# Two second-layer steps split by high and low parts, and Relus, casts and subtractions of the first tiles reordered

## The chip, the core and the metric

The kernel runs on one core of a Trainium2 chip. The core has five engines with queues of their own, each working in order: TensorE (PE, matrix products into PSUM; PEld are its weight loads), VectorE (DVE), ScalarE (ACT), GpSimd (POOL) and SyncE (SP, which here issues every DMA). They wait for each other by semaphores alone. The metric is the device time of one execution in microseconds; less is better.

## What is computed

A window attention with 8 batches, 8 heads, 576 positions and head width 64, and behind it a feed-forward layer of 4608 tokens:

```python
scores = scale * np.matmul(q, k.transpose(0, 1, 3, 2))
mask = (rel >= 0) & (rel < 64)
attn = softmax(np.where(mask, scores, -1e9))
x = np.matmul(attn, v)          # (4608, 512)
h = x @ w_in                    # 512 -> 2048
r = np.maximum(h, 0.0)
g = r * r
return g @ w_out                # 2048 -> 512
```

The weights arrive as 64-bit numbers, which the kernel reads as two 32-bit words each and turns into 32-bit ones.

## The kernel before

Twelve tiles of 384 tokens. The first four are "plain" tiles; the change lies in the first two (t = 0 and 1), whose work is interleaved with loading and converting the weights. All of it is one program in straight line, in an order written out by hand: the string `order` holds tokens such as `M11` or `p10a`, an operation's letter, a number, and sometimes the engine (d VectorE, a ScalarE, p GpSimd). A loop walks through the string and issues each token's instructions, so the string sets the order in every engine's queue. From tile 2 on a planner sets the order, and the change does not touch it.

To have enough precision, every 32-bit operand of a matmul is split into a high part (a rounded cast) and a low part (the number minus the high part), and a product is three: high by high, high by low, low by high.

The operations, with their lines:

- Weight block f (128 of the 2048 columns; 16 blocks): `w` fetches it (L105, L107); `a` takes the absolute value of the upper words (ScalarE, L121); `b` clamps and shifts it (VectorE, two instructions, L123 and L124); `c` and `d` put in the lower words and the sign (VectorE, L126, L128); `h` casts to the high part (ScalarE, L132); `l` subtracts it for the low part (VectorE, L135). The blocks use two staging buffers `a` in turn: `a` of block f can run when `l` of block f-2 is done.
- Step n = (tile, block): 34 steps in an order that `steps` holds. `M` is the first layer's product, 12 matmuls into PSUM bank 4 (L407), always the same bank. `r` is the Relu from that bank into one of two buffers `r` (ScalarE, L416), `p` the square in place (ScalarE here, L419), `g` the cast to the high part into one of three buffers (ScalarE, L424), `G` the subtraction for the low part into one of two buffers (VectorE, L426). `O` is the second layer's product, 9 matmuls of 512 columns into three banks (`mm2`, L445 to L450): first three with (high, high), then three with (high, low), at the end three with (low, high), so only the last three need `G`. `i` and `I` are an `O` in two pieces.
- So M of one step can begin when r of the step before has emptied bank 4; r of step n when G of step n-2 has read the buffer; G of step n when O of step n-2 has read the low half.
- Attention of a section i (a third of a tile): `S` scores (TensorE, L238), `o`, `s` mask, `z`, `y` maximum, `e`, `f` exponentials (ScalarE, L266), `k`, `R`, `m` division by the sum (`m` on GpSimd, L275), `X` transposes (TensorE, L279), `x` into SBUF, `V` values (TensorE, L301), `H` and `Q` high and low part of x. `T`, `U` transpose q and k of the first positions (TensorE, L199), `t`, `u` copy the result (L205). U2 and U3 use the same bank, so U3 needs u2 done.

Of the kernel before, what the change touches and what calls it, by code (L numbers as in the profile page):

```python
# [29 lines left out]
def window_attention_relu2_ffn(ctx: ExitStack, tc: tile.TileContext, q, k, v, w_in, w_out, out):  # L30
# [399 lines left out]
    def in_turn(x):  # L430
        return x.rearrange("p (a b) -> p b a", a=2)
# [49 lines left out]
    steps = [(t, f) for t in range(2) for f in range(AHEAD)]  # L481
    n0 = n1 = AHEAD
    while n1 < NF:
# [8 lines left out]
        L0 K5 P0 L1 P1 T1 t1d T0 t0a J0 j0 Y0 S0 o0a T2 t2a s0 z0 y0d T3 t3d J1 L2 K2 S1 j1 e0 o1a T4 t4a v0 w1 Y1 L3 v1  # L492
        N0 f0 K2 T5 d0 k0p t5a h0 s1 K5 z1 y1d S2 R0 m0d e1 l0 o2a X0 K5 x0 V0 s2 f1 k1p T6 z2 w2 R1 a1 b1 m1p X1 H0a Q0
        c1 t6a v2 L4 N1 y2p K2 f2 T7 t7a x1 S3 e2 d1 o3a s3 V1 k2p R2 U0 z3 h1 H1a u0a K4 l1 Q1
        m2p X2 U1 x2 w3 v3 a2 b2 K3 c2 y3p f3 u1a V2 T8 T9 H2a Q2 t8a t9a d2 S4 e3 o4a k3d R3 h2 s4 M0 U2 r0 u2a l2 p0a v4 z4
        U3 u3a a3 m3p X3 x3 b3 g0 G0 M1 c3 r1 p1a y4p S5 o5a w4 v5 s5 d3 f4 e4 w5 w6 g1 G1 V3 H3a k4p R4 z5 Q3
        h3 l3 a4 M2 r2 p2a O0 b4 O1 w7 v6 m4p X4 x4 c4 M3 g2 G2 V4 y5p e5 f5 k5p r3 H4a p3a g3 R5 d4 h4 a5 Q4
        w8 O2 G3 l4 m5p X5 x5 M4 a6 V5 w9 w10 w11 i3 r4 p4a g4 b5 H5d Q5 b6 M5 I3 r5 p5a c5 d5 w12 M6 w13 G4 O4
        h5 g5 r6 p6a c6 g6 M7 w14 d6 h6 w15 v7 v8 G5 O5 l5 r7 p7a a7 q0 M8 G6 O6 g7 l6 a8 r8 M9 b7 c7 d7 h7 G7 r9 O7
        p8a g8 p9a g9 M10 b8 c8 d8 G8 O8 l7 h8 r10 M11 l8 G9 a9 p10a g10 O9 a10 r11 p11a b9 c9 b10 M12 g11 G11  # L500
        O11 G10 r12 p12a M13 O10 q1 B0 c10 d9 h9 g12 d10 h10 r13 p13a l9 l10 a11 M14 a12 G12 r14 O12 M15 b11 B1
        B2 c11 B3 g13 G13 p14a r15 d11 h11 g14 O13 b12 c12 B4 M16 G14 p15a g15 r16 d12 h12 O14 p16a g16 l11 a13
        B5 B6 B7 l12 G15 M17 r17 a14 p17a O15 M18 G16 O16 b13 c13 r18 M19 d13 b14 g17 G17 O17 c14 h13 p18a l13
        g18 G18 O18 d14 r19 M20 a15 p19a b15 g19 G19 h14 l14 r20 O19 c15 d15 p20a g20 M21 G20 B8 B9 D0 q2 O20 h15 l15 r21
# [45 lines left out]
    with tc.manual_schedule(engines={E.PE, E.DVE, E.Activation, E.Pool, E.SP}):  # L550
        for token in order.split():
            op, eng = token[0], token[-1] if token[-1] in "dap" else None
            n = int(token[1:].rstrip("dap"))
            if op in "LN":
                load_first("LN".index(op), n)
            elif op == "v":
                load_v(*divmod(n, (NB + 1) // 2))
            elif op == "w":
                fetch_w(n)
            elif op == "q":  # L560
                load_qk(1 + n // NPAIR, n % NPAIR)
            elif op == "D":
                turn(1 + n // NPAIR, n % NPAIR)
            elif op in "TU":
                ps_f[op, n] = turn_first("TU".index(op), *divmod(n, 2))
            elif op in "tu":
                copy_first("tu".index(op), *divmod(n, 2), ps_f[op.upper(), n], copier(eng))
            elif op == "K":
                idle(n)
            elif op == "P":  # L570
                fetch_w(0, n)
            elif op in "JjY":
                weight("abc"["JjY".index(op)], 0, half=n)
# [694 lines left out]
    for s in range(NP * FULL + 2):  # L1268
        if s < NP * FULL:
            for mark in marks.get(2 * s, []):  # L1270
                mark()
            for n in range(7):
# [3 lines left out]
                if s < LAST and s % 2 == 0 and n % 2 == 0 or s == FAST_END + 1 and n % 2 == 0:  # L1276
                    f = s // 2 * 2 % NP * 2 + n // 2
# [61 lines left out]
```

## Time and profile before

| | |
|---|---|
| median of 3 runs | 840.22 us (840.2 to 841.16) |
| the profiled execution | 841.01 us, its span 839.3 us |
| TensorE busy | 825.5 us, 98% of the span |
| VectorE busy | 620.4 us, 74% |
| ScalarE busy | 434.8 us, 52% |
| GpSimd busy | 242.7 us, 29% |
| mean granted TensorE clock | 0.998 of full speed |

The span goes from the first to the last instruction; the execution's own time is a little longer. Busy times are averages over stages with different limits: the first 100 us are the stage that the change touches. Matmuls are pipelined, so that the events of one engine overlap a little; the start of an event minus the start of the one before is what a group of matmuls really takes.

### The profile page before, as it was taken

Reading aid. Unit: us, or ns where it says so; the run is one execution under the profiler, and the core shown is the slowest. Engines: PE = TensorE matmul, PEld = TensorE weight load, DVE = VectorE, ACT = ScalarE, POOL = GpSimd, SP = SyncE. Lnnn points to the kernel's source line nnn. Section 1 sums busy time; section 2 is a strip of 40 time slices with the busy share of each in tenths; the row PEclk is TensorE's granted clock in tenths of the full one; section 3 lists DMA queues with packets and bytes.
Section 4 is the critical chain, followed back from the end, with each engine's and each line's share of the span. In section 5 each row is a group of like instructions: output and inputs, shape, how many; then the busy total and the mean of one; then the engine's idle time right before and its main releaser. Section 6 shows DMA issues by size and latency. Waiting matters only on the chain.

```text
span 839.3 us, 18283 instructions
## 1 busy us (share of the span) xinstructions
PE 825.5 (98%) x6926; PEld 763.5 (91%) x6926; DVE 620.4 (74%) x908; ACT 434.8 (52%) x1181; POOL 242.7 (29%) x313
## 2 busy tenths in 40 slices
PE   8799999999999999999999999999999999999998
PEld 6689899889999999999999999999999999999997
DVE  6999997567656867867777866788766769566876
ACT  6796774656447554544452455344355425455441
POOL 1220003014647520311251334252233462202121
PEclk9999999999999999999999999999999999999999
DMA  9999945737598884999897898999895766889742
GB/s 225 246 343 273 357 176 88 140 116 182 142 197 259 219 175 114 312 243 219 180 307 235 215 229 175 260 289 231 272 286 151 256 213 183 250 263 309 242 168 76
DMA packets 292264, 184.99 MB, mean 220 GB/s; under 512 B 191184, under 2 KB 257488, under 8 KB 290128
## 3 DMA queue, kind: packets, MB, share of 16 engines
q1 hardware_dynamic: 292176, 183.81, 78.9%
q8 instruction: 55, 0.90, 0.5%
q14 instruction: 33, 0.27, 0.1%
HBM read 142.87 MB, written 40.89 MB: 219 GB/s over the span
## 4 chain that ended last, share of the span: by engine, by line
PE 92%; ACT 3%; DVE 3%; issue 1%; DMA 0%; SPq 0%; POOL 0%; ACTq 0%; DVEq 0%; POOLq 0%
PE banks L940 26%; PE banks L1038 24%; PE banks L407 14%; PE banks L449 13%; PE banks L1189 5%; PE banks L238 4%; PE banks L301 3%; PE banks L279 2%; ACT sel L266 1%; ACT a L121 1%; DVE a L126 1%; DVE w L135 0%; DMA w<-in_k_dram 0%; PE banks L199 0%; DVE a L123 0%
## 5 line engine op out<-in xcount | busy, mean ns | idle before, releaser
L1038 PE MATMUL banks<-w 128*128 128x512 f32 x888 | 199.8, 381 | 0.0
L1038 PEld LDWEIGHTS banks<-w 128*128 128x128 f32 x888 | 165.9, 189 | 21.6
L407 PE MATMUL banks<-x,w 128*128 128x384 f32 x768 | 138.9, 331 | 0.4 <-ACT r L416 0.3
L449 PE MATMUL banks<-w,g 128*128 128x512 f32 x576 | 136.1, 382 | 0.0
L407 PEld LDWEIGHTS banks<-x,w 128*128 128x128 f32 x768 | 127.2, 190 | 5.1 <-ACT r L416 2.0
L940 PE MATMUL banks<-x,w 128*128 128x384 f32 x768 | 130.3, 326 | 0.0
L940 PEld LDWEIGHTS banks<-x,w 128*128 128x128 f32 x768 | 125.6, 189 | 0.0
L449 PEld LDWEIGHTS banks<-w,g 128*128 128x128 f32 x576 | 106.4, 189 | 13.3 <-issue 0.3
L266 ACT ACTIVATE sel<-sel,nm 128x64 f32<-128x64 f32 x272 | 90.8, 336 | 22.6 <-DVE nm L260 22.2
L940 PE MATMUL banks<-w 128*128 128x384 f32 x576 | 100.7, 329 | 0.0
L970 POOL TENSOR_TENSOR g<-g 128x384 f32<-128x384 f32 x48 | 46.5, 972 | 181.5 <-ACT g L981 173.6
L940 PEld LDWEIGHTS banks<-w 128*128 128x128 f32 x576 | 93.4, 189 | 1.6
L1045 DVE TENSOR_TENSOR w<-w,banks 128x512 f32<-128x512 f32 (+1 forms) x61 | 41.1, 677 | 41.7 <-PE banks L1038 41.5
L416 ACT ACTIVATE r<-banks 128x384 f32<-128x384 f32 x64 | 31.1, 487 | 66.7 <-PE banks L407 61.2
L275 POOL TENSOR_TENSOR sel<-sel,nm 128x512 f32<-128x512 f32 x33 | 37.3, 1130 | 83.3 <-ACT g L981 32.8
L539 POOL TENSOR_TENSOR a<-w 128x256 f32<-128x256 f32 x28 | 24.3, 886 | 104.5 <-DVE w L135 74.7
L426 DVE TENSOR_TENSOR g<-r,g 128x384 fp32r<-128x384 f32 x64 | 38.2, 600 | 21.4 <-ACT g L424 14.6
L1022 ACT CAST w<-w 128x512 fp32r<-128x512 f32 x37 | 23.0, 621 | 56.4 <-PE banks L1038 56.4
L266 ACT ACTIVATION_READ_ACCUMULATOR sel<-sel,nm 128x1 f32 x272 | 51.2, 188 | 0.0
L958 DVE TENSOR_TENSOR w<-banks,r 128x384 f32<-128x384 f32 x64 | 38.3, 598 | 11.7 <-PE banks L940 11.2
L283 DVE TENSOR_TENSOR pt<-banks,masks 128x1024 f32<-128x1024 f32 x33 | 40.2, 1219 | 8.2 <-PE banks L279 8.2
L421 DVE TENSOR_TENSOR r<-r 128x384 f32<-128x384 f32 x38 | 24.9, 655 | 26.2 <-ACT r L416 26.1
(167 smaller groups left out, 1269.1 us busy)
## 6 DMA issues: line engine op xcount, KB each, us to landing
w<-mixed SPq DMA_DIRECT2D x128, 256.0 KB, 5.6
w<-kept SPq DMA_DIRECT2D x114, 256.0 KB, 6.1
w<-kept SPq DMA_DIRECT2D x52, 512.0 KB, 7.4
kept<-w SPq DMA_DIRECT2D x16, 1024.0 KB, 8.5
vt<-in_v_dram SPq DMA_DIRECT2D x144, 64.0 KB, 3.5
w<-in_moe_w_in_dram SPq DMA_DIRECT2D x16, 512.0 KB, 6.9
w<-in_moe_w_out_dram SPq DMA_DIRECT2D x16, 512.0 KB, 7.1
raw<-in_q_dram SPq DMA_DIRECT2D x112, 72.0 KB, 3.0
```

Of the source, the lines that this page charges most:

```text
L266: act.activation(sels[i][:, w, hd], sels[i][:, w, hd], AF.Exp, bias=nms[i][:, n], scale=SCALE, accum_out=sums[i][:, n])
L275: (dve if eng == "d" else pool).tensor_tensor(p, p, rs[i][:, :, None].broadcast_to([P, SW * 2, QB]), ALU.mult)
L283: dve.tensor_tensor(pts[i].rearrange("p (w n) q -> p w n q", n=2), ps_t[i][:, :, None, :].broadcast_to([P, SW, 2, P]), masks.rearrange("p ...
L407: pe.matmul(h_ps, lhsT=weights(kk, part), rhs=in_turn(x[xx][:, kk // 2, kk % 2]), start=n == 0, stop=n == 3 * NK - 1)
L426: (pool if eng == "p" else dve).tensor_tensor(gs[n][1], rg.pop(n), gs[n][0].bitcast(F32), ALU.subtract)
L449: pe.matmul(acc(t, tb), lhsT=gg[:, tb * P:(tb + 1) * P], rhs=in_turn(weights(part)), start=f == 0 and n == 0, stop=f == NF - 1 and n == 2)
L940: pe.matmul(ps[:, :TT], lhsT=w[:, part, kk * P:(kk + 1) * P], rhs=in_turn(x[:, xx, kk]), start=n < 4 and m == 0, stop=m == 5, skip_group_c ...
L958: plan("dve", 0.6, lambda: dve.tensor_tensor(to(), ps, other(), ALU.add), [kps, ko], keys, 0, after)
L970: plan("pool", 0.95, lambda: pool.tensor_tensor(x(), x(), x(), ALU.mult), [], keys)
L1038: pe.matmul(ps[:, :DM // parted], lhsT=gg[:, m // 2, m % 2], rhs=in_turn(wo_slot(w[m])[:, part, cols]), start=m == 0 and n == 0, stop=m == ...
L1045: plan("dve", 0.72 / parted, lambda ps=ps, to=to: dve.tensor_tensor(by_half(to()), by_half(to()), ordered(ps[:, :DM // parted]), ALU.add), ...
L1189: pe.matmul(ps[:, x * 2 * P:(x + 1) * 2 * P], lhsT=gg[:, st, x * P:(x + 1) * P], rhs=in_turn(w[:, st, part]), start=c == 0, stop=c == 5, s ...
```

## The change

Two things. `mm2` takes the list of products to make, and the tokens `i` and `I` now mean, for all blocks but the last, the two products with the high part (six matmuls over all three banks) and the one with the low part (three matmuls); before, they meant the first two token blocks and the third. And the string is reordered from the section with M0 on to M15.

```diff
-    def mm2(t, f, ghi, glo, weights, blocks=range(NTB)):
-        parts3 = list(enumerate(((ghi, 0), (ghi, 1), (glo, 0))))
+    def mm2(t, f, ghi, glo, weights, blocks=range(NTB), which=range(3)):
+        parts3 = [x for x in enumerate(((ghi, 0), (ghi, 1), (glo, 0))) if x[0] in which]
...
-        m2p X2 U1 x2 w3 v3 a2 b2 K3 c2 y3p f3 u1a V2 T8 T9 H2a Q2 t8a t9a d2 S4 e3 o4a k3d R3 h2 s4 M0 U2 r0 u2a l2 p0a v4 z4
-        U3 u3a a3 m3p X3 x3 b3 g0 G0 M1 c3 r1 p1a y4p S5 o5a w4 v5 s5 d3 f4 e4 w5 w6 g1 G1 V3 H3a k4p R4 z5 Q3
+        m2p X2 U1 x2 w3 v3 a2 b2 K3 c2 y3p f3 u1a V2 T8 T9 H2a Q2 t8a t9a d2 S4 e3 o4a k3d R3 m3p h2 s4 M0 X3 U2 a3 r0 p0a u2a
+        l2 v4 z4 U3 u3a x3 b3 g0 G0 M1 c3 r1 p1a g1 y4p S5 o5a w4 v5 d3 s5 f4 e4 w5 w6 G1 z5 V3 H3a k4p R4 Q3
...
-        w8 O2 G3 l4 m5p X5 x5 M4 a6 V5 w9 w10 w11 i3 r4 p4a g4 b5 H5d Q5 b6 M5 I3 r5 p5a c5 d5 w12 M6 w13 G4 O4
+        w8 O2 i3 G3 l4 m5p X5 x5 M4 a6 b5 V5 I3 w9 w10 w11 r4 p4a g4 H5d Q5 b6 M5 i4 r5 p5a c5 G4 d5 w12 M6 w13 I4
...
-        p8a g8 p9a g9 M10 b8 c8 d8 G8 O8 l7 h8 r10 M11 l8 G9 a9 p10a g10 O9 a10 r11 p11a b9 c9 b10 M12 g11 G11
-        O11 G10 r12 p12a M13 O10 q1 B0 c10 d9 h9 g12 d10 h10 r13 p13a l9 l10 a11 M14 a12 G12 r14 O12 M15 b11 B1
+        p9a g9 M10 b8 c8 G8 d8 O8 l7 h8 r10 M11 G9 l8 a9 r11 O9 p11a b9 g11 G11 p10a c9 g10 G10 M12 O11 d9
+        r12 p12a a10 M13 O10 q1 B0 h9 r13 b10 g12 l9 c10 d10 h10 p13a l10 a11 M14 a12 G12 r14 O12 M15 b11 B1
...
             elif op in "OiI":
+                last = steps[n][1] == NF - 1
                 mm2(*steps[n], *(gs[n] if op == "i" else gs.pop(n)), lambda part, f=steps[n][1]: wparts[f][:, 1, part],
-                    {"O": range(NTB), "i": range(2), "I": range(2, NTB)}[op])
+                    {"O": range(NTB), "i": range(2), "I": range(2, NTB)}[op] if last else range(NTB),
+                    range(3) if last or op == "O" else range(2) if op == "i" else range(2, 3))
```

The number of instructions stays the same. The orders on GpSimd and SyncE do not change, and from M15 on those of the other engines do not either.

TensorE around X5 (the L279 row), in the order before, with V4 ahead, O2 (x9), M4, V5, the first part of step 3 (x6), M5, the rest of step 3 (x3), M6:

```order
L301 MATMUL banks<-pt,vt 64x64 x24
L449 MATMUL banks<-w,g 128x512 x9
L279 MATMUL banks<-ident,sel 128x128 x4
L407 MATMUL banks<-x_322,w 128x384 x12
L301 MATMUL banks<-w,vt 64x128 x8
L301 MATMUL banks<-w,vt 64x64 x16
L449 MATMUL banks<-w,g 128x512 x6
L407 MATMUL banks<-x_629,w 128x384 x12
L449 MATMUL banks<-w,g 128x512 x3
L407 MATMUL banks<-x_629,w 128x384 x12
```

The same place in the order of the changed kernel:

```order
L301 MATMUL banks<-pt,vt 64x64 x24
L449 MATMUL banks<-w,g 128x512 x15
L279 MATMUL banks<-ident,sel 128x128 x4
L407 MATMUL banks<-x_322,w 128x384 x12
L301 MATMUL banks<-w,vt 64x128 x8
L301 MATMUL banks<-w,vt 64x64 x16
L449 MATMUL banks<-w,g 128x512 x3
L407 MATMUL banks<-x_630,w 128x384 x12
L449 MATMUL banks<-w,g 128x512 x6
L407 MATMUL banks<-x_630,w 128x384 x12
```

Six matmuls of step 3 moved ahead of X5 and stand with O2 as 15; three are left between V5 and M5; behind M5 six of step 4 take the place of step 3's rest.

ScalarE, in the order before, from h8 on: h8, r10, a9, p10, g10, a10, r11, p11, g11, r12, p12, h9:

```order
L132 CAST w<-a 128x2x512
L416 ACTIVATE r<-banks 128x384
L121 ACTIVATE a<-w 128x1024
L419 ACTIVATE r<-r 128x384
L424 CAST g<-r 128x384
L121 ACTIVATE a<-w 128x1024
L416 ACTIVATE r<-banks 128x384
L419 ACTIVATE r<-r 128x384
L424 CAST g<-r 128x384
L416 ACTIVATE r<-banks 128x384
L419 ACTIVATE r<-r 128x384
L132 CAST w<-a 128x2x512
```

The same place in the changed kernel: h8, r10, a9, r11, p11, g11, p10, g10, r12, p12, a10, h9:

```order
L132 CAST w<-a 128x2x512
L416 ACTIVATE r<-banks 128x384
L121 ACTIVATE a<-w 128x1024
L416 ACTIVATE r<-banks 128x384
L419 ACTIVATE r<-r 128x384
L424 CAST g<-r 128x384
L419 ACTIVATE r<-r 128x384
L424 CAST g<-r 128x384
L416 ACTIVATE r<-banks 128x384
L419 ACTIVATE r<-r 128x384
L121 ACTIVATE a<-w 128x1024
L132 CAST w<-a 128x2x512
```

r11, p11 and g11 moved ahead of p10 and g10, and a10 moved from ahead of r11 to behind p12.

VectorE, in the order before, from G9 on: G9, b9, c9, b10, G11 and G10, c10, d9 and d10, l9 and l10, G12:

```order
L426 TENSOR_TENSOR g<-r,g 128x384
L123 TENSOR_SCALAR a<-a 128x1024
L124 TENSOR_SCALAR a<-a 128x1024
L126 SCALAR_TENSOR_TENSOR a<-w,a 128x1024
L123 TENSOR_SCALAR a<-a 128x1024
L124 TENSOR_SCALAR a<-a 128x1024
L426 TENSOR_TENSOR g<-r,g 128x384 x2
L126 SCALAR_TENSOR_TENSOR a<-w,a 128x1024
L128 SCALAR_TENSOR_TENSOR a<-w,a 128x1024 x2
L135 TENSOR_TENSOR w<-a,w 128x2x512 x2
L426 TENSOR_TENSOR g<-r,g 128x384
```

The same stretch in the changed kernel, behind G9, l8 and b9: G11, c9, G10, d9, b10, l9, c10, d10, l10, G12:

```order
L426 TENSOR_TENSOR g<-r,g 128x384
L126 SCALAR_TENSOR_TENSOR a<-w,a 128x1024
L426 TENSOR_TENSOR g<-r,g 128x384
L128 SCALAR_TENSOR_TENSOR a<-w,a 128x1024
L123 TENSOR_SCALAR a<-a 128x1024
L124 TENSOR_SCALAR a<-a 128x1024
L135 TENSOR_TENSOR w<-a,w 128x2x512
L126 SCALAR_TENSOR_TENSOR a<-w,a 128x1024
L128 SCALAR_TENSOR_TENSOR a<-w,a 128x1024
L135 TENSOR_TENSOR w<-a,w 128x2x512
L426 TENSOR_TENSOR g<-r,g 128x384
```

G11 moved ahead of c9, d9 ahead of b10, and b10, l9, c10, d10, l10 now follow one another where the two blocks 9 and 10 stood side by side.

## Rows read from the trace of the kernel before

**Rows 1.** From the page: the span, the busy times of the engines (us, share of the span, instructions), and the chain of work that ended last by engine.
```profile
span 839.3 us, 18283 instructions
...
PE 825.5 (98%) x6926; PEld 763.5 (91%) x6926; DVE 620.4 (74%) x908; ACT 434.8 (52%) x1181; POOL 242.7 (29%) x313
...
PE 92%; ACT 3%; DVE 3%; issue 1%; DMA 0%; SPq 0%; POOL 0%; ACTq 0%; DVEq 0%; POOLq 0%
```

**Rows 2.** TensorE's events in order of time, 35 to 70 us: start, us, engine, line, operation, operands, count, and in brackets the idle time before and what ended it. In turn: M0, the second half of U2 and U3 (that is U3; what it waits for is u2), M1, X5, the six matmuls of step 3 (i3), M5 and M7.
```profile
35.72 3.37 PE L407 MATMUL banks<-x,w 128*128 128x384 f32 x12
...
39.94 0.46 PE L199 MATMUL banks<-ident,w 64*128 64x64 f32 x4 [0.46 <-ACT w L205]
...
40.74 2.20 PE L407 MATMUL banks<-x,w 128*128 128x384 f32 x12
...
57.59 0.66 PE L279 MATMUL banks<-ident,sel 128*128 128x128 f32 x4 [1.29 <-POOL sel L275]
...
61.33 1.56 PE L449 MATMUL banks<-w,g 128*128 128x512 f32 x6
...
62.73 2.11 PE L407 MATMUL banks<-x,w 128*128 128x384 f32 x12
...
69.42 2.11 PE L407 MATMUL banks<-x,w 128*128 128x384 f32 x12
```

**Rows 3.** ScalarE's events in order of time, the same columns: r0 and u2 at 39 us, g3 at 56 us.
```profile
39.12 0.49 ACT L416 ACTIVATE r<-banks 128x384 f32<-128x384 f32 x1 [1.47 <-PE banks L407]
...
39.52 0.37 ACT L205 COPY w<-banks 128x256 f32<-128x256 f32 x1
...
56.03 0.51 ACT L424 CAST g<-r 128x384 fp32r<-128x384 f32 x1
```

**Rows 4.** The second half of the fetch of weight block 3 on SyncE's queue (start, us), the time from its issue to its landing by the view of that line, and GpSimd's products m4 and m5 (start, us).
```profile
30.54 0.50 SPq L107 DMA_DIRECT2D w<-in_moe_w_out_dram  x1
...
DMA to landing us min/median/max: 6.5/6.5/6.5
...
48.54 1.05 POOL L275 TENSOR_TENSOR sel<-sel,nm 128x512 f32<-128x512 f32 x1 [0.86 <-DVE nm L272]
...
55.51 2.02 POOL L275 TENSOR_TENSOR sel<-sel,nm 128x512 f32<-128x512 f32 x1 [0.39 <-DVE nm L272]
```

**Rows 5.** VectorE's events in order of time, 82 to 103 us: d8; G11 and G10; d9 and d10; l9 and l10; the first of the two instructions of b11; c11; G13.
```profile
82.03 1.44 DVE L128 SCALAR_TENSOR_TENSOR a<-w,a 128x1024 int32<-128x1024 int32 x1
...
90.76 1.02 DVE L426 TENSOR_TENSOR g<-r,g 128x384 fp32r<-128x384 f32 x2
...
93.14 2.92 DVE L128 SCALAR_TENSOR_TENSOR a<-w,a 128x1024 int32<-128x1024 int32 x2
...
95.92 2.47 DVE L135 TENSOR_TENSOR w<-a,w 128x1024 fp32r<-128x1024 f32 x2
...
99.53 0.69 DVE L123 TENSOR_SCALAR a<-a 128x1024 f32<-128x1024 f32 x1 [0.68 <-ACT a L121]
...
100.99 1.49 DVE L126 SCALAR_TENSOR_TENSOR a<-w,a 128x1024 int32<-128x1024 int32 x1
...
102.41 0.53 DVE L426 TENSOR_TENSOR g<-r,g 128x384 fp32r<-128x384 f32 x1
```

**Rows 6.** ScalarE's events in order of time, 83 to 102 us: h8, a10, r11, r12, h10, r13, p13, a11 and a12 together, r14.
```profile
83.50 1.04 ACT L132 CAST w<-a 128x1024 fp32r<-128x1024 f32 x1 [1.41 <-DVE a L128]
...
87.47 1.58 ACT L121 ACTIVATE a<-w 128x1024 f32<-128x1024 f32 x1
...
88.95 0.48 ACT L416 ACTIVATE r<-banks 128x384 f32<-128x384 f32 x1
...
91.88 0.49 ACT L416 ACTIVATE r<-banks 128x384 f32<-128x384 f32 x1 [1.35 <-DVE g L426]
...
96.08 1.04 ACT L132 CAST w<-a 128x1024 fp32r<-128x1024 f32 x1
...
97.04 0.48 ACT L416 ACTIVATE r<-banks 128x384 f32<-128x384 f32 x1
...
97.55 0.52 ACT L419 ACTIVATE r<-r 128x384 f32<-128x384 f32 x1
...
97.98 3.00 ACT L121 ACTIVATE a<-w 128x1024 f32<-128x1024 f32 x2
...
100.81 0.56 ACT L416 ACTIVATE r<-banks 128x384 f32<-128x384 f32 x1
```

**Rows 7.** TensorE's events in order of time, 84 to 104 us: M11, M12, O12, M15.
```profile
84.99 2.21 PE L407 MATMUL banks<-x,w 128*128 128x384 f32 x12
...
89.48 2.22 PE L407 MATMUL banks<-x,w 128*128 128x384 f32 x12 [0.33 <-ACT r L416]
...
99.63 2.11 PE L449 MATMUL banks<-w,g 128*128 128x512 f32 x9
...
101.57 2.11 PE L407 MATMUL banks<-x,w 128*128 128x384 f32 x12
```

**Rows 8.** Stretches (from:to in us): their length, the busy time of PE, PEld, DVE, ACT and POOL with instruction counts in brackets, the granted TensorE clock (1.00 is full speed), DMA share and GB/s.
```profile
36.00:37.00 1.00, 1.00 (x4) 1.00 (x4) 0.97 (x4) 0.82 (x2) 0.00 (x0) 0.50 0.73 102
...
56.00:57.00 1.00, 0.30 (x2) 0.00 (x0) 1.00 (x2) 0.84 (x2) 1.00 (x1) 1.00 1.08 363
...
100.00:120.00 20.00, 20.00 (x110) 18.68 (x109) 19.41 (x22) 14.62 (x23) 0.00 (x0) 1.00 0.69 287
```

More of the change, by code (lines that the diff above doesn't have):

```diff
@@ L494, in window_attention_relu2_ffn @@
         c1 t6a v2 L4 N1 y2p K2 f2 T7 t7a x1 S3 e2 d1 o3a s3 V1 k2p R2 U0 z3 h1 H1a u0a K4 l1 Q1
-        m2p X2 U1 x2 w3 v3 a2 b2 K3 c2 y3p f3 u1a V2 T8 T9 H2a Q2 t8a t9a d2 S4 e3 o4a k3d R3 h2 s4 M0 U2 r0 u2a l2 p0a v4 z4
-        U3 u3a a3 m3p X3 x3 b3 g0 G0 M1 c3 r1 p1a y4p S5 o5a w4 v5 s5 d3 f4 e4 w5 w6 g1 G1 V3 H3a k4p R4 z5 Q3
-        h3 l3 a4 M2 r2 p2a O0 b4 O1 w7 v6 m4p X4 x4 c4 M3 g2 G2 V4 y5p e5 f5 k5p r3 H4a p3a g3 R5 d4 h4 a5 Q4
-        w8 O2 G3 l4 m5p X5 x5 M4 a6 V5 w9 w10 w11 i3 r4 p4a g4 b5 H5d Q5 b6 M5 I3 r5 p5a c5 d5 w12 M6 w13 G4 O4
-        h5 g5 r6 p6a c6 g6 M7 w14 d6 h6 w15 v7 v8 G5 O5 l5 r7 p7a a7 q0 M8 G6 O6 g7 l6 a8 r8 M9 b7 c7 d7 h7 G7 r9 O7
-        p8a g8 p9a g9 M10 b8 c8 d8 G8 O8 l7 h8 r10 M11 l8 G9 a9 p10a g10 O9 a10 r11 p11a b9 c9 b10 M12 g11 G11
-        O11 G10 r12 p12a M13 O10 q1 B0 c10 d9 h9 g12 d10 h10 r13 p13a l9 l10 a11 M14 a12 G12 r14 O12 M15 b11 B1
+        m2p X2 U1 x2 w3 v3 a2 b2 K3 c2 y3p f3 u1a V2 T8 T9 H2a Q2 t8a t9a d2 S4 e3 o4a k3d R3 m3p h2 s4 M0 X3 U2 a3 r0 p0a u2a
+        l2 v4 z4 U3 u3a x3 b3 g0 G0 M1 c3 r1 p1a g1 y4p S5 o5a w4 v5 d3 s5 f4 e4 w5 w6 G1 z5 V3 H3a k4p R4 Q3
+        h3 l3 a4 M2 r2 p2a O0 b4 O1 w7 v6 m4p X4 x4 c4 M3 g2 G2 V4 y5p e5 f5 k5p r3 H4a p3a g3 d4 R5 h4 a5 Q4
+        w8 O2 i3 G3 l4 m5p X5 x5 M4 a6 b5 V5 I3 w9 w10 w11 r4 p4a g4 H5d Q5 b6 M5 i4 r5 p5a c5 G4 d5 w12 M6 w13 I4
+        g5 r6 h5 p6a c6 g6 M7 w14 d6 h6 w15 v7 v8 G5 O5 l5 r7 p7a a7 q0 M8 G6 O6 g7 l6 r8 a8 M9 b7 c7 p8a g8 G7 r9 d7 h7 O7
+        p9a g9 M10 b8 c8 G8 d8 O8 l7 h8 r10 M11 G9 l8 a9 r11 O9 p11a b9 g11 G11 p10a c9 g10 G10 M12 O11 d9
+        r12 p12a a10 M13 O10 q1 B0 h9 r13 b10 g12 l9 c10 d10 h10 p13a l10 a11 M14 a12 G12 r14 O12 M15 b11 B1
         B2 c11 B3 g13 G13 p14a r15 d11 h11 g14 O13 b12 c12 B4 M16 G14 p15a g15 r16 d12 h12 O14 p16a g16 l11 a13
```

## The prediction

> **What bounds the kernel now.** I read the page first, its busy times and its chain [rows 1]: TensorE is busy 825.5 of 839.3 us and holds 92% of the chain that ends last. So the end moves only if TensorE waits less, or waits anew. Then I read TensorE's row of events over the stretch that the change touches, looking for the idle times in brackets. Between 35 and 70 us there are two: 0.46 us before the second of two transposes U3, and 1.29 us before X5 [rows 2]. Between 80 and 102 us there is one, 0.33 us before M12, put down to ScalarE's Relu r11 [rows 7]. From 100 to 120 us TensorE is busy 20.00 of 20.00 us [rows 8]: behind the reordered stretch nothing is idle that could take up a delay. VectorE is busy 19.41 us of the same 20; its queue is nearly full, so a wait added there is not easily made good. The question is therefore which of TensorE's waits go, and what the new order makes VectorE and ScalarE wait for.
>
> **The change, part by part.** All tokens are named as in the section on the kernel; a time "after" is worked out by carrying the rows' durations through the new order.
>
> *U3 and M1, 39 to 41 us.* X3 is put ahead of U2 and U3, and a3 ahead of r0. a3 needs ScalarE, which is idle until r0 at 39.12 (idle 1.47 before it), and words that were issued at 30.54 and took 6.5, so lie there at 37.04 [rows 3, 4]. One a takes 1.4 to 1.5 (two of them 2.83 to the next Relu [rows 6]), so it is hidden in that idle time. Now the copy u2 stands behind r0 and p0: r0 39.12, p0 39.62, u2 at about 40.05, 0.37 long, U3 at 40.47 instead of 39.94, M1 at 40.86 instead of 40.74. Cost 0.1 us. If a3 were to find its words late, r0 would move with it by up to its own 1.4: bounds 0 and 1.4, I take 0.1 since the landing has a row.
>
> *The gap at X5, 56 to 69 us.* The first six matmuls of step 3 (i3) now follow O2 and fill the gap; they need g3. g3 begins at 56.03 in the rows, 0.1 later here, and takes 0.51: 56.66. i3 takes 1.3 to 1.4 (61.33 to 62.73 in the rows), so X5 starts at 58.0 instead of 57.59 [rows 2, 3]. Then M4 and V5 as before, 0.2 to 0.4 later. But between V5 and M5 only three matmuls stand now instead of six: M5 at about 62.4 instead of 62.73, held there by H5 on VectorE, which follows V5. What follows M5 has 0.7 us less to do, since step 3 is complete: M7 at 68.35 where it was 69.42. Gain 1.0 us here. It hangs on X5's own input, the GpSimd product, which took 2.02 us there and 1.05 us elsewhere [rows 4]; it starts 0.9 later because d4 goes first. At 1.05 it ends under i3; at 2.02 it costs X5 0.5 us more. Bounds of the gain: 0.5 and 1.0.
>
> *M11 and M12, 80 to 90 us.* G7 and G8 are put ahead of d7 and d8. A G costs 0.5 (two of them 1.02 [rows 5]), so d8 ends some 0.3 later than in the rows, h8 starts at 83.8 instead of 83.50, r10 behind it at 84.75, and M11, which needs the bank that r10 empties, at 85.3 instead of 84.99 [rows 6, 7]. TensorE could have been there 1.0 before its old time, at 84.0: the gain is waited away. Then a small gain: r11 no longer stands behind a10 (87.47, r11 at 88.95 [rows 6]), so M12 follows O9 without the 0.33: 85.3 + 2.05 + 1.95 = 89.3, against 89.48.
>
> *O12 and M15, 89 to 105 us: the term that decides.* Before, a10 ran at 87.47, ahead of r11. Now a10 stands behind r11, p11, g11, p10, g10, r12 and p12 on ScalarE, and on VectorE G11 stands ahead of c9, and c9 ahead of G10. G11 writes the same low half that O9 reads, so it cannot start before O9 ends, at 89.5; and r12 writes the buffer that G10 reads (in the rows, too, r12 waits 1.35 for a G [rows 6]). From G11 on one thing waits for the other, down to the Relu r14 that frees the bank for M15. By the rows [rows 5, 6]: G11 0.50 and G10 0.50 (half of two), c9 1.42 (c11 at 100.99, G13 at 102.41), r12 to p12 0.51 (r13 at 97.04, p13 at 97.55), p12 to a10 0.43 (p13, a11 at 97.98), a10 to b10 1.55 (a11, b11 at 99.53), b10 1.46 (b11, c11), l9 1.23 (half of two), c10 and d10 1.46 each (half of two d), h10 0.96 (96.08 to r13), p13 0.43, a11 and a12 2.83 (97.98 to r14 at 100.81), and r14 to M15 0.53 (as r11 at 88.95 to M12 at 89.48). The sum is 15.3 us, so M15 starts at 89.5 + 15.3 = 104.8. On TensorE six groups lie between M12 and M15, at 1.94 to 1.95 each (O12 at 99.63, M15 at 101.57 [rows 7]): 11.7 us, done at 101.0. So TensorE waits 3.8 us in two pieces: before the last three matmuls of O12, which need G12 (behind l10, about 102.3), and then before M15. Against 101.57 in the rows that is 3.2 us late. Bounds: the rows of c and d differ by 0.04 (1.46 and 1.42); so much less on each of fifteen links is 0.6, so 2.6; with M11 late by another 0.5, 3.7.
>
> *Behind it.* b11 starts at 102.9 instead of 99.53 and r14 at 104.2 instead of 100.81: all three engines are 3.2 to 3.4 us late, in the old order from there on. Nothing is idle on TensorE that would give it back [rows 8]. Sum: +3.2 us.
>
> **Against which time.** The profiled execution took 841.01 us, its span 839.3; 841.01 + 3.2 = 844.2. It lies 0.8 above the median of the three runs; on 840.22 the sum gives 843.4.
>
> **The rivals.**
>
> *The late chain does not bind, and the filled gap remains (not slower).* The place is X5, the price what reached M7: -1.0, or -0.5 if M11 takes half. It decides at r14: if it is ready by 101 us, the links from G11 to M15 would have to take 11.5 us instead of 15.3. For it: the dependencies between buffers could be looser than I read them. Against it: each link has a row. Time 839.2 to 839.7; chance 0.12, mostly no change.
>
> *All the named waits go (faster).* 0.46 + 1.29 + 0.33 [rows 2, 7], 2.1 us, and M14 no wait either: 838.1. It needs r10, r11 and r14 all in time. Chance 0.08.
>
> *Half of the chain is hidden.* If VectorE's and ScalarE's instructions run 0.15 us shorter per link or G11 is let go earlier, 1 to 2 us of the 3.8 go: 841.0 to 842.5. Chance 0.12.
>
> *The clock falls in the new gap.* In the rows of stretches the granted clock is 0.50 at 36 to 37 us [rows 8], the lower of the two levels; ahead of that TensorE had run small matmuls with idle times between them. There the twelve matmuls of M0 took 3.37 us, where M1's took 2.20 [rows 2]. Against it: at 56 to 57 us TensorE is busy 0.30 of 1 us and the clock stays 1.00 [rows 8]. The new gap, 3.8 us with three matmuls in it, is longer than any idle time in the rows here. If it brings such a spell, 1.2 us come on top: 844.6, up to 845.6 with the longer bound. Chance 0.25. The Trainium skill (page "TensorE: Matmul & The Clock Gate", section "Part 1: The HAM clock gate") calls half clock the resting state, to which an engine without activity falls back; by that rule the spell would follow this gap, and the row at 36 us agrees with it, while the short gap at 56 us shows no such fall.
>
> **How the numbers follow.** Chances: the chain without a clock spell 0.43 (842.6 to 844.1), with one 0.25, half hidden 0.12, not slower 0.12, faster 0.08. I predict the first, 843.4 us. A measurement of this kernel can tell about 0.2% from no change, 1.7 us. Slower by more than that: 0.43 + 0.25 + half of 0.12, about 0.75. Within it: the other half and nearly all of the not-slower case, about 0.16. Faster: 0.09. For 8 in 10 the range takes the first two cases, the half-hidden one and the edge of the not-slower one: 840.6 to 845.6. The forecast's own range is 842.6 to 844.1.
>
> **What would show it.** In the profile after: X5 without idle time behind i3, and M7 about 1 us earlier; then a wait of about 1.3 us before M11 for r10; on VectorE idle times before G11, b10 and l10 of 1 us or more each; about 2 us before O12's last three matmuls, and M15 at about 104.8. If M15 stands near 101, the fourth part is wrong, and if M11 is at 84, the third. If the granted clock shows 0.5 behind 103 us, the clock case holds. A time below 841.9 would make the forecast wrong.

## The result, and the profile after

The changed kernel takes 844.95 us (median of 6 runs, 844.78 to 848.98) against 840.25 for the kernel before (6 runs, 839.89 to 841.16): ratio 1.0065, 95% interval 1.0046 to 1.0084. It is slower, as forecast, but by 4.7 us and not by the sum's 3.2. The profiled execution took 846.72 us, 1.8 over the median; its span is 845.0. One execution of the kernel before (867.17 us) and one of a version further down (1073.19 us) were slow as a whole, at mean granted clocks of 0.948 and 0.755, and stand in no ratio here.

The page of the changed kernel, the lines that answer to [rows 1]:

```profile
span 845.0 us, 18286 instructions
...
PE 828.0 (98%) x6926; PEld 764.9 (91%) x6926; DVE 621.2 (74%) x908; ACT 433.9 (51%) x1181; POOL 242.9 (29%) x313
...
PE 87%; DMA 4%; SPq 3%; DVE 2%; ACT 2%; issue 1%; ACTq 0%
```

Busy times stand within 0.4% of before: the kernel does the same work. The chain is what changed: in this execution it runs for 7% through transfers and SyncE's queue. TensorE's events, 36 to 73 us (columns as in [rows 2]): M0, X3, U3, M1, O2 with the six matmuls of step 3, X5, M7:

```profile
36.27 2.22 PE L407 MATMUL banks<-x,w 128*128 128x384 f32 x12
39.40 0.66 PE L279 MATMUL banks<-ident,w 128*128 128x128 f32 x4 [0.91 <-POOL w L275]
...
41.76 0.46 PE L199 MATMUL banks<-ident,w 64*128 64x64 f32 x4 [1.32 <-ACT w L205]
42.15 3.20 PE L407 MATMUL banks<-x,w 128*128 128x384 f32 x12
...
57.13 3.65 PE L449 MATMUL banks<-w,g 128*128 128x512 f32 x15
60.61 0.60 PE L279 MATMUL banks<-ident,sel 128*128 128x128 f32 x4
...
71.22 2.22 PE L407 MATMUL banks<-x,w 128*128 128x384 f32 x12
```

X5 no longer waits. But ahead of M1 stand 2.23 us of waiting where there were 0.46, and M1 itself takes 3.20 us instead of 2.20. Why, the chain of waits in order of time says (start, us, what), 32 to 42 us:

```profile
32.75 6.47 DMA w<-in_moe_w_out_dram
39.28 0.04 issue
39.32 1.20 ACT a L121
40.52 0.38 ACT r L416
40.92 0.52 ACT r L419
41.45 0.27 ACT w L205
41.72 0.04 issue
41.76 0.47 PE banks L199 x4
```

It is read downward: the fetch of weight block 3 lands at 39.22, a3 starts then, r0, p0 and u2 stand behind it, and U3 needs u2. TensorE's events, 87 to 107 us, answering to [rows 7]: M11, M12, O12 in two pieces, M15:

```profile
87.80 2.22 PE L407 MATMUL banks<-x,w 128*128 128x384 f32 x12 [0.74 <-ACT r L416]
...
91.79 2.11 PE L407 MATMUL banks<-x,w 128*128 128x384 f32 x12
...
101.53 1.46 PE L449 MATMUL banks<-w,g 128*128 128x512 f32 x6
105.39 0.92 PE L449 MATMUL banks<-w,g 128*128 128x512 f32 x3 [2.41 <-DVE g L426]
106.74 2.22 PE L407 MATMUL banks<-x,w 128*128 128x384 f32 x12 [0.43 <-ACT r L416]
```

And the chain behind these waits. VectorE (against [rows 5]): G11, c9, b10, l10:

```profile
92.06 0.56 DVE L426 TENSOR_TENSOR g<-r,g 128x384 fp32r<-128x384 f32 x1 [1.53 <-ACT r L419]
92.54 1.42 DVE L126 SCALAR_TENSOR_TENSOR a<-w,a 128x1024 int32<-128x1024 int32 x1
...
97.05 0.69 DVE L123 TENSOR_SCALAR a<-a 128x1024 f32<-128x1024 f32 x1 [1.19 <-ACT a L121]
...
103.65 1.23 DVE L135 TENSOR_TENSOR w<-a,w 128x1024 fp32r<-128x1024 f32 x1 [1.17 <-ACT w L132]
```

ScalarE (against [rows 6]): r12, a10, h10, a11 and a12, r14:

```profile
94.51 0.49 ACT L416 ACTIVATE r<-banks 128x384 f32<-128x384 f32 x1 [1.90 <-DVE g L426]
...
95.47 1.56 ACT L121 ACTIVATE a<-w 128x1024 f32<-128x1024 f32 x1
...
102.57 1.04 ACT L132 CAST w<-a 128x1024 fp32r<-128x1024 f32 x1 [3.82 <-DVE a L128]
...
103.94 2.37 ACT L121 ACTIVATE a<-w 128x1024 f32<-128x1024 f32 x2
106.17 0.52 ACT L416 ACTIVATE r<-banks 128x384 f32<-128x384 f32 x1
```

The row puts G11's wait down to a square on ScalarE. Of the things that G11 needs, ScalarE's cast g11 ends at 91.64 us, while O9 on TensorE starts at 89.85 and takes 2.10; so O9 ends last, at 91.95, as the forecast has it. From G11's start to a11's start the chain takes 11.88 us, 11.91 by the forecast's links. From M12 to M15 it is 14.95 us (106.74 less 91.79) against 12.09 before.

Stretches of one us (columns as in [rows 8]), in and behind M1's waits and behind M15's start:

```profile
41.00:42.00 1.00, 0.24 (x4) 0.24 (x4) 1.00 (x2) 0.70 (x2) 0.23 (x1) 1.00 1.11 389
42.00:43.00 1.00, 1.00 (x9) 0.93 (x8) 0.96 (x3) 0.74 (x2) 0.00 (x0) 1.00 0.99 366
43.00:44.00 1.00, 1.00 (x6) 1.00 (x5) 1.00 (x3) 0.04 (x1) 0.00 (x0) 0.61 1.17 216
44.00:45.00 1.00, 1.00 (x5) 0.84 (x3) 1.00 (x1) 0.00 (x0) 0.00 (x0) 0.50 0.74 177
45.00:46.00 1.00, 1.00 (x18) 0.72 (x20) 0.97 (x2) 0.58 (x2) 0.00 (x0) 0.50 1.11 373
...
107.00:108.00 1.00, 1.00 (x8) 1.00 (x8) 1.00 (x1) 0.51 (x2) 0.00 (x0) 1.00 1.00 418
```

The granted clock fell to the lower of the two levels, but in this execution behind M1's wait, not behind the gap at O12. (It was low once more ahead of M0, 0.50 from 23 to 26 us.)

### The profile page after: what moved, and what is told of

Same layout as the page of the kernel before. It is cut to its first block, busy times and chain, and to the rows that moved or that the text cites. A ratio compares the mean times of both kernels' runs of the same rounds, so it can differ in the third digit from the quotient of the medians.

```text
span 845.0 us, 18286 instructions
## 1 busy us (share of the span) xinstructions
PE 828.0 (98%) x6926; PEld 764.9 (91%) x6926; DVE 621.2 (74%) x908; ACT 433.9 (51%) x1181; POOL 242.9 (29%) x313
## 4 chain that ended last, share of the span: by engine, by line
PE 87%; DMA 4%; SPq 3%; DVE 2%; ACT 2%; issue 1%; ACTq 0%
PE banks L942 26%; PE banks L1040 24%; PE banks L449 12%; PE banks L407 12%; PE banks L1191 5%; PE banks L238 4%; PE banks L301 3%; DMA w<-in_moe_w_out_dram 2%; PE banks L279 2%; DMA vt<-in_v_dram 1%; DMA w<-in_moe_w_in_dram 1%; SPq L160 1%; SPq L188 1%; DVE a L128 1%; SPq L107 1%
```

## The experiments

Two theories stood against each other: that all of the loss is the late chain to M15, the rest being chance; and that the first section's a3 and X3 cost as well, because what covered a3 was no property of the kernel. M0's start shifts from execution to execution by what TensorE waits for ahead of it (35.2 to 38.7 us in the profiles here), so places are given from M0's start. Diffs show the moved piece of the order only.

**The change in three parts**, and the whole once more, on one chip. The first two order lines of the diff alone (head), the next two (mid: the split of steps 3 and 4), the last three (tail).

> The kernel before with the first two changed lines alone (X3 ahead of U2, a3 ahead of r0, m3, G1 and others moved with them). Theory A, my sum: a3 is hidden in ScalarE's idle time and M1 loses 0.1 us; the time is that of before within 0.3 us. Theory B, a3 stands before its words have landed or after a late h8-like cast (h2), so that r0, u2 and U3 follow late and M1 starts 1 to 1.5 us late: 841.2 to 841.8, and another 1 us if the clock falls in that wait as in the profile of the changed kernel.

> The kernel before with the middle part alone: d4 ahead of R5, steps 3 and 4 split by high and low part, i3 in the gap before X5. Theory 1: the 1.0 us that is won up to M7 is waited away at M11, where r10 stands behind h8 and h8 behind d8 on a full VectorE: 840.0 to 840.4. Rival: VectorE is not the limit there, and the gain stays: 839.2 to 839.5.

> The kernel before with the last three changed lines of the order alone (r8 ahead of a8 up to M15), nothing else changed. Theory 1, the chain from G11 over c9, G10, r12, a10, b10, l9, c10, d10, h10, a11, a12 to r14: M15 comes about 15.3 us after O9 ends, and 3.0 to 3.4 us later than before; the time is 843.2 to 843.7 against 840.2. Theory 2, the loss sits in the head of the reordering (a3, X3, U3) and the chain only inherits a late start: under 1 us.

> All three parts, that is the changed kernel once more, on the chip of the other three. If the parts add up, its difference to before is the sum of theirs; it took 844.95 us in the first measurement, so 4.4 to 5.0 us above before. Theory 3, the profiled execution's head start late and its clock spell are chance: its profile then shows other waits ahead of M1 than the first one.

The times of the kernel before are from 18 executions on that chip, its last three columns from the profile of [rows 2, 7].

| kernel | median us | ratio to before (interval) | M1 from M0 | M10 to M11 | M12 to M15 |
|---|---|---|---|---|---|
| before | 840.09 | | 5.02, M0 at half clock | 3.89 | 12.09 |
| head | 843.12 | 1.0036 (1.0023 to 1.0048) | 5.51 | 3.89 | 12.06 |
| mid | 840.08 | 0.9997 (0.9988 to 1.0006) | 4.18 | 3.89 | 12.06 |
| tail | 844.06 | 1.0050 (1.0036 to 1.0063) | 4.13 | 4.11 | 14.91 |
| whole | 845.29 | 1.0062 (1.0050 to 1.0075) | 5.41 | 4.72 | 14.91 |

The tail holds the chain, and it is as long there as in the whole. The head, which the forecast priced at 0.1, costs 3.0 by itself, and the mid nothing. Alone they add up to 7.0, together they cost 5.2. Head and tail each lie a little over what was expected of them (842.2 to 842.8 with a clock spell, and 843.2 to 843.7). Where the mid's gain goes shows TensorE's row of the mid kernel: M0, M1, X5, M7:

```profile
35.41 2.22 PE L407 MATMUL banks<-x,w 128*128 128x384 f32 x12
...
39.59 2.20 PE L407 MATMUL banks<-x,w 128*128 128x384 f32 x12
...
56.84 0.60 PE L279 MATMUL banks<-ident,sel 128*128 128x128 f32 x4
...
68.46 2.22 PE L407 MATMUL banks<-x,w 128*128 128x384 f32 x12 [1.00 <-ACT r L416]
```

X5 does not wait, and 1.00 us is given back at M7, where ScalarE does r6 behind the long h5. M0 runs at full clock here, and M1 follows it by 4.18. ScalarE's row at that place, h2 and r0:

```profile
37.04 1.05 ACT L132 CAST w<-a 128x1024 fp32r<-128x1024 f32 x1 [0.44 <-DVE a L128]
37.99 0.48 ACT L416 ACTIVATE r<-banks 128x384 f32<-128x384 f32 x1
```

r0 follows h2 without idle time, where the kernel before had 1.47 us [rows 3]: behind a full-clock M0 there is nothing to hide a3 in.

**a3 alone, twice.**

```diff
-M0 U2 r0 u2a
+M0 U2 a3 r0 u2a
...
-U3 u3a a3 m3p X3
+U3 u3a m3p X3
```

> The kernel before with one edit: the first section's Relu a3 goes ahead of r0 on ScalarE. Theory 1 (the cover was the half-clock M0 of one profiled execution): where M0 runs at full clock ScalarE follows from h2 to r0 without idle time, so a3 (1.05 to 1.2 us) pushes r0, p0, u2a and u3a, and U3 and M1 start about 1.0 us later against M0's start than in mid_only (M1 5.2 behind M0 against 4.18): 841.0 to 841.5. Theory 2 (the sum of the prediction): the idle time before r0 covers it, +0.1 at M1, 840.2 to 840.4. Theory 3 (a3 costs only through X3's place): M1 as in mid_only, 840.1.

> a3_only once more, word for word, for a second profiled execution. Theory 1: where its M0 runs at full clock (2.2 us), r0 stands behind a3 and M1 comes 5.0 to 5.2 us behind M0 against 4.18 in mid_only; where M0 runs at half clock (3.3 us), M1 stands at 5.0, as in the kernel before. The median stays 0.8 to 1.3 us over the kernel before. Theory 2 (a3 is hidden at either clock): at full clock M1 at 4.2, and the median within 0.3 us of the kernel before.

First: 842.29 us (840.54 to 844.47), before 840.84 on that chip, ratio 1.0015 (1.0003 to 1.0026). Second: 843.23 (842.64 to 843.28), before 840.00, ratio 1.0038 (1.0025 to 1.0051). The two profiles fell on either side of the question. The first, M0, U3, M1:

```profile
35.66 3.34 PE L407 MATMUL banks<-x,w 128*128 128x384 f32 x12
...
39.85 0.46 PE L199 MATMUL banks<-ident,w 64*128 64x64 f32 x4 [0.46 <-ACT w L205]
...
40.65 2.20 PE L407 MATMUL banks<-x,w 128*128 128x384 f32 x12
```

M0 at half clock: M1 4.99 behind it, to be set beside 5.02 before: a3 costs nothing. The second, the same three:

```profile
35.71 2.22 PE L407 MATMUL banks<-x,w 128*128 128x384 f32 x12
...
40.71 0.63 PE L199 MATMUL banks<-ident,w 64*128 64x64 f32 x4 [2.39 <-ACT w L205]
...
42.03 3.27 PE L407 MATMUL banks<-x,w 128*128 128x384 f32 x12
```

and a3 on ScalarE there:

```profile
38.88 1.14 ACT L121 ACTIVATE a<-w 128x1024 f32<-128x1024 f32 x1 [0.51 <-DMA w<-in_moe_w_out_dram]
```

M0 at full clock: a3 waits 0.51 for its words (issued at 31.82, 7.0 on the way), r0 and u2 stand behind it, U3 waits 2.39 us, M1 comes 6.32 behind M0 and runs at half clock. That is more than the 5.0 to 5.2 expected: the price has three parts (a3's length, a late landing, a clock spell), where the theory had one. The times, too, lie over the 841.0 to 841.5 expected. From M0's start on, this execution is 3.2 us behind the mid kernel's at M2 and 2.9 at the end of the span. So a3 alone can make up the whole of the head's loss (843.12); the two medians (1.45 and 3.23 over before) do not agree on how often it does.

**X3 alone.**

```diff
-R3 h2 s4 M0 U2
+R3 m3p h2 s4 M0 X3 U2
```

> The kernel before with one edit: X3 stands right behind M0, ahead of U2, and GpSimd's order that feeds it (m3's part behind R3) goes with it. Theory 1: X3 waits about 0.95 us for GpSimd's w, U2 stands behind it, and M1 comes 0.4 to 0.7 us later against M0's start than in mid_only: 840.5 to 840.9. Theory 2: the time that X3 stands in front of U3 is taken from U3's own wait, M1 as in mid_only, 840.1.

840.80 us (840.21 to 843.39), before 840.84, ratio 1.0008 (0.9997 to 1.0019). X3 waits 0.99 for GpSimd and M1 stands 5.11 behind M0, 0.93 later than in the mid kernel; at M15 0.54 of it is left. A loss of some 0.5 us in the profile; the time does not resolve it.

**Is it the landing?** The fetch of block 3 put ahead of two pairs of q and k blocks on SyncE's queue, with a3 as above.

```diff
-c1 t6a v2 L4
+c1 t6a v2 w3 L4
```

> a3_only with w3's two fetches two pairs of transfers earlier in SyncE's queue (the q and k blocks that stood ahead of them come behind them). Theory 1 (part of a3's price is the landing of w3's second half, which came 0.51 us after ScalarE stood ready in a3_again and made U3's wait 2.39 us and M1 a half-clock one): a3 waits for no transfer, U3's wait is 0.5 to 1.2 us, M1 5.0 to 5.2 behind M0 in the profile, and the runs lie below a3_again's 842.6 to 843.3, at 841.0 to 841.8, if the later q and k blocks do not start M0 later. Theory 2 (the landing does not matter): the runs stay at 842.3 to 843.3 with M1 6 us or more behind M0 in those at full clock.

845.17 us (844.26 to 848.14), ratio 1.0058 (1.0036 to 1.0080): the proviso struck. TensorE waited 2.17 us for a q block, M0 began at 38.74, and ran at half clock (3.90 us). So most of this loss lies ahead of M0, which began 3.3 us later than in the mid kernel. a3 follows h2 without a wait, and M1 is 5.56 behind M0, but with that M0 this says nothing on the full-clock case. The share of the landing in a3's price stays open; shown is only that it is there in two of the four full-clock profiles with a3 first (0.41 and 0.51 us).

**The chain to M15, link by link.** The tail kernel, first with c9 ahead of G11, then also with a10 ahead of r12:

```diff
-b9 g11 G11 p10a c9 g10 G10 M12 O11 d9 r12 p12a a10 M13
+b9 c9 g11 G11 p10a g10 G10 M12 O11 d9 r12 p12a a10 M13
...
-g10 G10 M12 O11 d9 r12 p12a a10 M13
+g10 a10 G10 M12 O11 d9 r12 p12a M13
```

> tail_only with one edit: on VectorE c9 stands ahead of g11 and G11. Theory 1 (the chain from G11 over c9, G10, r12, p12, a10 to M15 sets the 14.9 us from M12 to M15): the chain loses G11's time, some 1.4 us, M12 to M15 about 13.5, 842.4 to 842.9 beside tail_only's 844.06. Theory 2 (another chain, that of O9's landing over G11, bears as much): M12 to M15 stays at 14.5 to 14.9 and the time at 843.7 to 844.3.

> tail_c9 with a second edit: on ScalarE a10 goes ahead of r12, behind g10. Theory 1 (the 14.9 us from M12 to M15 come from two entries into the same chain: c9 behind G11, and a10 behind r12, which waits for M12's end): in tail_c9 a10 began right behind p12 although c9 was done early; now it begins some 2.3 us earlier, b10 some 1.8 us earlier, M12 to M15 falls from 14.4 to 12.4 to 12.9, near the 12.06 of mid_only, and the time to 841.5 to 842.3. Theory 2 (VectorE's work alone sets it): M12 to M15 stays at 14.0 or more and the time at 843.3 or more.

With c9 alone 844.22 us (843.21 to 848.40; ratio 1.0039, 1.0020 to 1.0058), M12 to M15 14.38. Half a microsecond went, not 1.4. ScalarE's row there shows why, r12, p12, a10:

```profile
94.27 0.49 ACT L416 ACTIVATE r<-banks 128x384 f32<-128x384 f32 x1 [1.32 <-PE banks L407]
94.79 0.53 ACT L419 ACTIVATE r<-r 128x384 f32<-128x384 f32 x1
95.22 1.50 ACT L121 ACTIVATE a<-w 128x1024 f32<-128x1024 f32 x1
```

r12 no longer waits for VectorE's G but for M12 itself, and a10 behind it: the chain has a second entry. With a10 moved as well, it begins at 91.74, M12 to M15 is 13.02 and the time 841.54 (840.96 to 843.78; ratio 1.0016, 1.0005 to 1.0027). Over the kernel before in the same measurement the medians are 3.97 us for the tail, 3.38 with c9 moved and 1.42 with both: two exchanges bring 2.5 us of the tail's loss back, the greater part by a10; M12 to M15 is still 0.96 longer than in the head and the mid, which no run here takes apart.

**Clock spells behind the gap at O12.** In the whole change's second profile M15 took 3.90 us, in the c9 kernel's 3.82, in the tail's 2.22. The tail with 16 multiplications in front of O12, into a bank that nothing reads (each shows as two rows):

```diff
-G12 r14 O12 M15
+G12 r14 K116 O12 M15
```

> tail_only with one edit: in front of O12, where TensorE waits 2.4 us for VectorE's g, it multiplies 128-column tiles into a free bank that nothing reads; no order changes. Theory 1 (part of the lost time is half-clock time of TensorE behind the new gap, in some executions): no half-clock stretch from 100 to 120 us, the runs lie closer together and the median falls to 843.0 to 843.5. Theory 2 (the chain alone sets the loss): the median stays at 843.8 to 844.3. If the multiplications delay O12 it would be 844.5 or more.

844.06 us (843.07 to 850.92; ratio 1.0040, 1.0024 to 1.0057). The median is the tail's own to the digit, but the kernel before took 840.84 in this measurement and 840.09 in the tail's. No spell in the profile; its O12 and M15:

```profile
98.68 3.73 PE L515 MATMUL banks<-ident 128*128 128x128 f32 x32
102.17 2.19 PE L449 MATMUL banks<-w,g 128*128 128x512 f32 x9
104.19 2.11 PE L407 MATMUL banks<-x,w 128*128 128x384 f32 x12
```

O12 does not wait any more, but it stands behind the multiplications as a whole: from M12 (88.94) to M15 are 15.25 us instead of 14.91. So the run does not settle it: it takes the gap away and makes the stretch longer, and its ratio (1.0040) lies below the tail's (1.0050) with intervals that overlap.

What the spells cost can be read elsewhere: the mean granted clock stands on record for every execution, not only for the profiled ones. The spell at M0 in the profile before makes it 0.998; 1.000 leaves room for less than 1 us of half clock (0.0005 of 840 us, twice). Of 93 executions of the kernel before, 63 show 1.000, with a median of 840.1 us, and 22 show 0.998, with 841.3. The mean does not say where a spell lies, but the execution that was profiled before the change belongs to the smaller group. All 11 executions of the mid show 1.000; all 7 of the head, all 5 of the tail and all 6 of the changed kernel's first measurement show 0.998 or less. The executions at 1.000 alone: X3 alone 840.6 (7), a3 alone 840.9 in its first measurement (4) and 843.2 in its second (1), the tail with the multiplications 843.5 (8), the whole change 844.4 (1). The kernel before takes 840.2 at 1.000 in that measurement. By these medians, of few executions, a3 and X3 alone cost 0.7 and 0.4 us without spells, and the tail some 3.3, of which 0.3 are the multiplications' own; the spells come on top. The single 843.2 shows that a3 can cost 3 us without a spell, too; no profile shows how.

**The change without its head.**

> The changed kernel without its first two order lines (the first section's a3, m3's part and X3 stand as before): the split of the second-layer steps together with the last three lines. Theory 1 (what the filled gap at X5 gives is waited away at M11, behind h8 and d8): M7 comes 0.7 to 1.0 us earlier against M0's start than in tail_only, M10 to M11 grows from 4.1 to about 4.9, M11 and M15 stand as in tail_only, 843.7 to 844.3. Theory 2 (the gain reaches the end): M15 0.7 to 1.0 earlier against M0's start, 843.0 to 843.3.

843.73 us (842.44 to 844.44; ratio 1.0043, 1.0031 to 1.0055). M10 to M11 is 4.75 with a wait of 0.69 for r10; the tail alone has 4.11. From M1 to M15 this kernel is 0.2 us faster than the tail: the mid's gain is waited away at M11, as expected.

**A version to beat both.** The mid, with the Relus that free TensorE's bank ahead of the long weight operations (r6 ahead of h5, r10 of h8, r11 of a10, and G8 of d8); then also u2a ahead of r0, G12 ahead of l9 and r14 ahead of a12; then the first with r13 ahead of h9, G12 and r14 (the last pair of the diff is this third version's):

```diff
-h5 g5 r6 p6a c6 g6
+g5 r6 h5 p6a c6 g6
...
-c8 d8 G8 O8 l7 h8 r10 M11 l8 G9 a9 p10a g10 O9 a10 r11
+c8 G8 d8 O8 l7 r10 h8 M11 l8 G9 a9 p10a g10 O9 r11 a10
...
-d9 h9 g12 d10 h10 r13 p13a l9 l10 a11 M14 a12 G12 r14
+d9 r13 h9 g12 d10 h10 p13a G12 l9 l10 a11 M14 r14 a12
```

> A version meant to beat both: the kernel before with the split around R5 and V5 (mid_only), and on ScalarE the Relus that free TensorE's bank go ahead of the long operations of the weight split (r6 ahead of h5, r10 ahead of h8, r11 ahead of a10), on VectorE G8 ahead of d8; VectorE's chain to M15 stays as before. Theory 1 (M7, M12 and M15 are set by those Relus): M7's wait of 1.0 us and M12's of 0.39 go, M15 comes 1.2 to 1.4 us earlier against M0's start than in mid_only, 838.7 to 839.2. Theory 2 (VectorE, busy without a gap there, sets M12 to M15): M7 earlier, M15 and the time as in mid_only, 840.1.

> mid_evac, and u2a ahead of r0 on ScalarE (U3 waits 0.77 us for it in mid_only), G12 ahead of l9 and l10 on VectorE and r14 ahead of a12 on ScalarE. Theory 1: U3 and M1 0.3 to 0.4 us earlier, M15 not held by r14, 838.3 to 838.9. Theory 2 (VectorE sets the time): as mid_only, 840.1; if r0, now behind u2a, holds M1 instead, nothing is gained at M1.

> mid_evac with r13 ahead of h9 on ScalarE (M14 waits 0.88 us for it in mid_evac), G12 ahead of l9 on VectorE and r14 ahead of a12. Theory 1 (the Relus set the time): M14 right behind O11, M15 63.5 to 63.8 us behind M0 against 64.50 in mid_evac and 65.0 to 65.3 without the edits, 838.6 to 839.3. Theory 2 (the time is set further on, by work that follows M15 and does not come earlier): M15 earlier, a new wait of TensorE behind it, 840.0 as before.

840.10 (ratio 1.0004, 0.9994 to 1.0014), 840.79 (1.0010, 0.9997 to 1.0023) and 840.63 us (1.0000, 0.9990 to 1.0011): none beats the kernel before. From M0 on, the first has M7 1.38 us earlier than the mid kernel, M12 2.01, M15 0.81, M18 0.81 (0.31 of each is there at M1 already, ahead of its edits). The third has M15 1.51 earlier and M18 only 0.25, and at the end of the span nothing. Its TensorE row behind M15 (O14 in two pieces) shows a new wait:

```profile
105.78 1.56 PE L449 MATMUL banks<-w,g 128*128 128x512 f32 x6
107.61 0.92 PE L449 MATMUL banks<-w,g 128*128 128x512 f32 x3 [0.27 <-DVE g L426]
```

The Relus set M7 to M12, but much of what was won there was waited away at the next Relu or G (M14 waits 0.88 for r13 in the first). VectorE's row in the mid kernel names one idle time from 49 to 97 us, 0.83 us at 72. That VectorE is what holds the rest is likely, but no run here takes work from it.

## Why the prediction was right and wrong

*The direction and the chain: right.* "O12 and M15, the term that decides" holds link by link in the rows of the changed kernel. Only a11 with a12 took 2.23 us to r14 instead of 2.83, so M12 to M15 is 14.91 to 14.95 and not 15.5. TensorE's wait in two pieces is 2.84 us, forecast 3.8. From M12 to M15 the stretch grew by 2.8 us (tail and whole). Two entries of the chain, c9 behind G11 and a10 behind r12, were shown by taking them away: 14.91, 14.38, 13.02.

*X5 and M11: right.* The gap is filled, M3 to M7 is 17.07 us instead of 18.32, M11 waits (0.74 us, 1.3 forecast), and next to nothing of the gain reaches M15 (0.2 us, the change without its head beside the tail). That the parts' medians add up to 7.0 and not to 5.2 is not explained by it: M11's wait for r10 is as long with the head (0.66 and 0.74) as without (0.69). Counted in the profiles from M0's start to the end of the span, head and tail are 2.4 and 3.2 us over the mid, and the whole 5.0 and 5.8, so there the parts nearly add up. The medians stand for few executions with different spells (the tail's profile has one of 3.4 us at 23 to 27 us, ahead of everything that it changes); how much of the 1.8 us this makes is not shown.

*U3 and M1: the step that failed.* "So it is hidden in that idle time. [...] Cost 0.1 us." The idle 1.47 us before r0 [rows 3] was real, but it was there because M0 took 3.37 us at half clock in the one execution that was profiled [rows 2, 8]; the prediction read both rows and used the spell as an argument on another step. In most executions M0 takes 2.22 us (11 of the 17 profiles here; 63 of 93 executions of the kernel before show a mean granted clock of 1.000, which leaves no room for such a spell) and ScalarE goes from h2 to r0 without idle time. There a3 costs its own length, and where the fetch lands late, more: with a3 first M1 came 1.2 to 2.1 us later from M0 on than in the mid kernel (in three of four such profiles together with X3, which alone makes 0.9), and where M1 then ran at half clock, M2 came another 1.1 to 1.6 later. The second cover, the landing at 37.04 [rows 4], was one execution's as well: in the 16 profiles with the same queue order this fetch was issued at 30.54 to 33.86 and took 5.3 to 9.1 us. The bound of 1.4 was there, but the value within it was taken from the wrong execution, X3's wait for GpSimd was put at nothing, and the clock rival stood at O12 alone.

*The clock: right as a rival, at another place.* M1 ran at half clock in three of the four profiles with a3 first and M0 at full clock (3.20, 3.27, 3.65 us; not in the whole change's second one), M15 in three of five with a wait of 1.8 to 2.4 us in O12. So the rival's place was hit as well, in some executions, and 844.95 lies within its 844.6 to 845.6; but that is partly luck, since those bounds do not hold the head's cost. By the Trainium skill (page "TensorE: Matmul & The Clock Gate", section "Part 1: The HAM clock gate") the number of slow matmuls at a kernel's start differs from run to run of the same kernel. M0 stands 36 us behind the start; that it was slow in 6 of 17 profiles here is the same kind of spread at a later place.

*"Nothing is idle that would give it back": right.* Behind M15 nothing came back. From M0's start to the end of the span the mid kernel takes 802.9 us, the head 805.4, the tail 806.1, the whole change 808.7 and 807.9. What is late at M15 is late at the end, and the tail loses more: it is 2.2 us behind the mid at M15, 2.8 at 153 us and 3.2 at the end, in steps of 0.1 to 0.4 without a named wait, and what these are stays open. That the tail's 3.2 equals the forecast's is therefore in part luck, since the sum had all of it at M15. With this 3.2 and the 1.1 that the head leaves at M15 where no spell precedes it (68.64 behind M0 in the whole change's second profile, 67.50 in the tail) the sum is 840.2 + 4.3 = 844.5; the one execution of the whole change at a mean granted clock of 1.000 took 844.4. For the last 0.4 there are the spells, at least one in each of the six executions behind 844.95; how it divides is not shown.

## What to carry to other kernels

An idle time is cover only if it is there in the executions that count: before an operation is hidden in one, look at what ends it, and whether that took its usual length; an engine at half clock makes false cover on all others. One profile cannot tell this, but the mean granted clock of the other executions can, as 1.000 did here in 63 of 93. Price an operation that is moved ahead of a Relu on an in-order engine at its full length first, and its transfer's landing at the latest one seen. And when a chain between engines is cut, look for its next entry: here c9 alone brought 0.5 of the 1.4 us, and both exchanges 1.9.

## What was not expected of the hardware

M0 ran at half clock in 6 of 17 profiled executions, and began anywhere from 35.2 to 38.1 us in the 16 whose fetches stand in the same order. The lower clock showed while TensorE was busy all of the time, after the sparse stretch: in the changed kernel TensorE is busy 1.00 from 42 us on, and the granted clock falls at 43 to 44 us. A fetch of 512 KB at the same place of the queue took 5.3 to 9.1 us from issue to landing in these 16.
